# Opening a block of the convolution's kernel behind both slots of a step, its matmul tasks due one step apart

## The chip, the cores and the metric

The kernel runs on one core of a Trainium2 chip. Its engines are TensorE (PE, with its weight loads PEld), VectorE (DVE), ScalarE (ACT), GpSimd (POOL) and SyncE (SP), which here only issues transfers. The metric is the device time of one execution in microseconds (us). Three runs of the kernel before gave 1361.73, 1362.64 and 1366.7 us; their median is 1362.64.

## The reference

Two heads work on separate inputs, and their outputs are set side by side. Head A is a convolution over 2048 positions and 448 channels by a state-space kernel K, made from 256 complex terms for each channel and applied by Fourier transforms. Head B is full softmax attention with 16 heads of 28.

```python
def A(u, log_A_real, A_imag, C_real, C_imag, log_dt, D_skip):      # u: 1 x 2048 x 448
    dt = exp(log_dt)
    A = -exp(log_A_real) + 1j * A_imag                              # 448 x 256
    C = (C_real + 1j * C_imag) * dt[:, None]
    P = exp((A * dt[:, None])[:, :, None] * pos[None, None, :])
    K = 2.0 * einsum("dn,dnl->dl", C, P).real                       # 448 x 2048
    y = irfft(rfft(u_t, 2 * L) * rfft(K, 2 * L), 2 * L)[:, :, :L]
    return y.transpose(0, 2, 1) + u * D_skip

def B(x, wqkv, wo):
    q, k, v = split(x @ wqkv)                                       # 16 heads of 28
    p = softmax(q @ k.T * 28 ** -0.5)
    return (p @ v) @ wo

return concatenate([A(...), B(...)], axis=-1)
```

## The kernel before

The kernel has a prelude and one long loop. The prelude (to about 258 us) projects q, k and v, and makes the first powers ("seeds") for K; both go through DRAM. The loop then runs over 256 steps (`NS`); each step is one tile of 128 keys (`kt`) for a group of four heads and 512 queries (`u`, of which there are 16). Instructions stand on every engine in the order in which the loop writes them.

What a step does is listed in `ORDER`, item by item:

- `m0` to `m3` (`max_mm`) are the four matmuls by which the maximum of later scores is found, 19 steps ahead. Each takes a PSUM tile from a ring of three buffers, called pm in the profile. m0 (weights times `kdif`) is read by a Relu on ACT into `rl`; m1 is joined with that by a custom operation on DVE (`rl<-pm,rl`); m2 and m3 are reduced on DVE (`mx<-pm`).
- `s0` to `s3` (`s_mm`) are the score matmuls into a ring of three other tiles, pss, each followed by the exp on ACT (`p<-pss`).
- `pv` (`pv_step`) multiplies the exps of the step before with v, into po.
- `f` is a slot: one narrow task is run there, if one is due. There are two slots in a step, one ahead of `pv` and one behind it; in the last steps there is a third. A task takes its PSUM tile from the ring pm as well.
- `v` runs the next of a block's nine g operations on DVE (`vec`).
- `k` first has the next block's factors loaded if the current block's powers are all issued (`k_next`), then opens a block if one is due (`k_begin`), and runs up to three of its nine e operations on POOL.

K is made in 56 blocks. A block is opened by `k_start`: three copies on ACT set the first elements of its tables g, e and of the factors zg (zg is one PSUM tile, in which the g operations also keep their scratch). Nine g operations on DVE (the first of them, `lowest`, is three instructions) and nine e operations on POOL then double the tables. After that come three matmul tasks: p0 and m1 (the code's name for p1 and a note that the block is done) multiply g by e, with one copy to `ko` each, and p2 transforms `ko`, with a copy to `yk` on ACT and a store. A block may be opened when its due step (3.5 steps for each block, `KP`) has come, the block two before it is done, and no powers are waiting. The three tasks are put into `m_due` at the opening, and come due `KD` = 5 steps later.

A slot takes the first of these that is due: an urgent task (the end of a maximum, `max_end`; the row sums and the scaling of a finished unit, `sums` and `scale`), an output projection, a task of `m_due`, a u task (a part of the forward transform of u: eight matmuls and one or two evictions on ACT, called ub; these last until step 102), or a task of the spectrum and of the inverse transform (from step 192 on). When all blocks are done, the PSUM pool of pm and zg is replaced by one with four buffers.

Of the kernel before, what the change touches and what calls it, by code (L numbers as in the profile page):

```python
# [30 lines left out]
NU = G * NQ  # L31
NS = NU * NK
LEAD = 3
ORDER = ('m0', 's0', 'm1', 's1', 'v', 'f', 'pv', 'k', 'f', 'v', 'm2', 's2', 'm3', 's3', 'v')
PB = 8
F1 = 2
FX, PD, GAP = 1, 2, 2
# [5 lines left out]
K0, KP, KD, UP = 0, 3.5, 5, 3  # L43
# [47 lines left out]
def body(ctx, tc, a, out):  # L91
# [526 lines left out]
    def k_start(b):  # L618
        sd = sds[b]
        e = g_p.tile([128, 2, 16, N2], F32, name="e", bufs=2)  # L620
        g = g_p.tile([128, 2, 16, N1], F32, name="g", bufs=2)
        zg = ps_g.tile([128, CQ], F32, name="zg")
        egs[b] = e, g
        zgs[b] = zg
        nc.scalar.activation(g[:, :, :, :4], sd[:, F_G:F_Z].rearrange("p (c h e) -> p c h e", c=2, e=4), AF.Copy)
        nc.scalar.activation(zg[:, :Z_G], sd[:, SDF - Z_G:], AF.Copy)
        nc.scalar.activation(e[:, :, :, :8], sd[:, :F_G].rearrange("p (c h e) -> p c h e", c=2, e=8), AF.Copy)

    def e_power(b, i, q):

        t, m = egs[b][0], 8 << i
        zz = sds[b][:, F_Z:].rearrange("p (k f h) -> p k f h", k=6, f=3)
        if q == 0:
            zr = zz[:, i, 0, :][:, None, :, None].to_broadcast([128, 2, 16, m])
            nc.gpsimd.tensor_tensor(t[:, :, :, m:2 * m], t[:, :, :, :m], zr, ALU.mult)
        elif q == 1:
            uts[0] = g_p.tile([128, 2, 16, 32], F32, name="eu")[:, :, :, :m]
            zi = zz[:, i, 1:3, :][:, :, :, None].to_broadcast([128, 2, 16, m])
            nc.gpsimd.tensor_tensor(uts[0], t[:, ::-1, :, :m], zi, ALU.mult)
        else:  # L640
            nc.gpsimd.tensor_tensor(t[:, :, :, m:2 * m], t[:, :, :, m:2 * m], uts[0], ALU.add)

    def g_powers(b):

        t, zg = egs[b][1], zgs[b]
        zz = zg[:, :Z_G].rearrange("p (k f h) -> p k f h", k=3, f=3)
        tt = nc.vector.tensor_tensor

        def first(i, m):
            tt(t[:, :, :, m:2 * m], t[:, :, :, :m], zz[:, i, 0, :][:, None, :, None].to_broadcast([128, 2, 16, m]), ALU.mult)  # L650

        def second(i, m, c):
            n = c.stop - c.start
            u = zg[:, CQ // 2:CQ // 2 + n * 16 * m].rearrange("p (c h m) -> p c h m", c=n, m=m)
            zi = zz[:, i, 1 + c.start:1 + c.stop, :][:, :, :, None].to_broadcast([128, n, 16, m])
            tt(u, t[:, ::-1, :, :m][:, c], zi, ALU.mult)
            return lambda: tt(t[:, c, :, m:2 * m], t[:, c, :, m:2 * m], u, ALU.add)
        both, u = slice(0, 2), {}

        def lowest():  # L660
            first(0, 4)
            second(0, 4, both)()
        ops = [lowest, lambda: first(1, 8), lambda: u.update(a=second(1, 8, both)), lambda: u["a"](), lambda: first(2, 16)]
        for c in (slice(0, 1), slice(1, 2)):
            ops += [lambda c=c: u.update(a=second(2, 16, c)), lambda: u["a"]()]
        return ops
# [3 lines left out]
    def k_mm(b):  # L670
        t_ = {}

        def part0(i):
            pw = w_tile()
            e, g = egs[b] if i == 0 else egs.pop(b)
            for n, (h, c) in enumerate(((0, 0), (0, 1), (1, 0), (1, 1))):
                for j in range(4):
                    x_ = h * 8 + i * 4 + j
                    nc.tensor.matmul(pw[32 * j:32 * j + 32, :N2], g[:, c, x_, :], e[:, c, x_, :],
                                     start=n == 0, stop=n == 3, tile_position=(0, 32 * j))  # L680
            if i == 0:
                t_["ko"] = g_p.tile([128, 2, N2], F32, name="ko", bufs=2)
            nc.scalar.activation(t_["ko"][:, i], pw[:, :N2], AF.Copy)

        def part1():
            ko = t_["ko"]
            pw = w_tile()
            for i in range(2):
                for c in range(2):
                    mm32(pw[64 * c:64 * c + 64, i * 128:(i + 1) * 128], ko[:, i, :], w1[:, c, :], True, True, 64 * c)  # L690
            yk = g_p.tile([128, N1, 4, 2], F32, name="yk", bufs=2)
            nc.scalar.activation(yk.rearrange("p k j i -> p i j k"),
                                 pw[:, :256].rearrange("p (i j k) -> p i j k", i=2, j=4), AF.Copy)
            nc.sync.dma_start(yk_d[b // NBF][:, :, b % NBF], yk.rearrange("p (m k) j i -> p m (k j i)", k=4))
        return [lambda: part0(0), lambda: part0(1), part1]
# [191 lines left out]
    m_due = collections.deque()  # L887
# [71 lines left out]
    def k_begin(s_):  # L959
        if not (k_due and K0 + k_due[0] * KP <= s_ and done["mm"] >= k_due[0] - 2 and not powers["e"] and not powers["g"]):  # L960
            return
        b = k_due.popleft()
        k_start(b)
        powers["g"] += g_powers(b)
        powers["e"] += [lambda i=i, q=q: e_power(b, i, q) for i in range(3) for q in range(3)]
        p0, p1, p2 = k_mm(b)

        def m1():
            p1()
            done["mm"] = b  # L970
        m_due.extend((s_ + KD, t_) for t_ in (p0, m1, p2))
        last[0] = b

    last = [None]
# [13 lines left out]
    for s in range(NS):  # L988
# [25 lines left out]
        ps = []  # L1014
        for op in ORDER:
            if op[0] == "s":
                ps.append(s_mm(u, kt, int(op[1])))
            elif op[0] == "f":
                slot(s)
            elif op[0] == "v":  # L1020
                vec()
            elif op == "k":
                k_next()
                k_begin(s)
                for _ in range(3):
                    if powers["e"]:
                        powers["e"].popleft()()
            elif op == "pv":
                if prev:
                    pv_step(*prev)  # L1030
                    if prev[1] == NK - 1:
                        fin(prev[0], s)
            elif sm < NS:
                max_mm(sm // NK, sm % NK, int(op[1]))
# [76 lines left out]
```

## Time and profile before

| what | before |
|---|---|
| median of three runs | 1362.64 us |
| the profiled execution, device time | 1363.72 us |
| its span in the profile | 1361.9 us |
| mean granted clock of TensorE | 0.976 |
| busy: PE / DVE / ACT / POOL | 1243.9 / 991.3 / 966.1 / 839.5 us |

The span is the time from the first to the last instruction of the program in the profile; the device time contains it and what lies around it. A line of grouped instructions gives the source line (here always L75, a helper that records every operation), the engine, the operation, the tiles that it writes and reads, the shape, the count, then busy time in us and the mean of one in ns, and last the idle time of that engine ahead of them with what ended it. A line of waits gives who waited for whom, the total in us, the number of times and the longest. A line of the chain of waits gives start, length and instruction; a line of the timeline gives start, length, engine and instruction, all in us.

### The profile page before, as it was taken

To read this page: it belongs to the slowest core of one execution; us is meant where nothing else is said; L and a number is where in the kernel's file an instruction comes from. 1 tells how busy PE (TensorE), PEld (TensorE's weight loads), DVE (VectorE), ACT (ScalarE), POOL (GpSimd) and SP (SyncE) were. 2 spreads that over 40 slices of the span, in tenths; PEclk is the share of its full clock that TensorE was granted. 3 is DMA by queue.
4 is the path that set the end of the run, shared out by engine and by line. 5 is a ranking of instruction groups with operands and counts; after the bars stand their busy time and mean duration, and the time that the engine had idled before them with its cause. 6 is when DMAs were issued, how large, how long until landed. Compare 5 with 4: busy or idle time off the path is not lost.

```text
span 1361.9 us, 33142 instructions
## 1 busy us (share of the span) xinstructions
PE 1243.9 (91%) x12625; PEld 709.8 (52%) x12625; DVE 991.3 (73%) x2138; ACT 966.1 (71%) x2067; POOL 839.5 (62%) x705
## 2 busy tenths in 40 slices
PE   6878885799999999999999999999998999998997
PEld 5657762455555555555555555555555545544433
DVE  5897886877777777777788888888887766857311
ACT  4876752488888888888888887878786655655553
POOL 3685681278877878878888988888895111202221
PEclk9988987899999999999999999999999999999999
DMA  6677669636675545378534233632325534636476
GB/s 197 199 261 266 225 212 271 179 74 150 147 164 118 128 135 159 111 202 198 162 94 97 56 73 86 146 79 67 79 65 140 189 116 161 206 111 203 138 192 176
DMA packets 200089, 205.36 MB, mean 151 GB/s; under 512 B 95993, under 2 KB 158521, under 8 KB 197881
## 3 DMA queue, kind: packets, MB, share of 16 engines
q1 hardware_dynamic: 199544, 201.13, 53.2%
q10 hardware_dynamic: 384, 2.10, 0.6%
q8 instruction: 100, 1.64, 0.5%
q14 instruction: 61, 0.49, 0.1%
HBM read 120.73 MB, written 82.18 MB: 149 GB/s over the span
## 4 chain that ended last, share of the span: by engine, by line
PE 61%; DVE 17%; ACT 12%; issue 3%; DMA 3%; POOL 3%; SPq 0%; ACTq 0%; DVEq 0%; POOLq 0%
PE pm L75 35%; PE po L75 13%; PE pss L75 12%; ACT p L75 6%; DVE mx L75 4%; DVE g L75 2%; DVE tri L75 2%; ACT rl L75 2%; DVE p L75 2%; POOL qhat L75 1%; DVE pr L75 1%; DVE zg L75 1%; DVE rl L75 1%; DVE sg L75 1%; ACT tri L75 1%
## 5 line engine op out<-in xcount | busy, mean ns | idle before, releaser
L75 ACT ACTIVATE p<-pss 128x512 f32<-128x512 f32 x1024 | 565.4, 609 | 138.5 <-PE pss L75 127.5
L75 PE MATMUL pss<-qhat,khat 128*128 128x512 f32 x1024 | 403.1, 400 | 3.3 <-ACT p L75 3.3
L75 DVE TENSOR_REDUCE mx<-pm 128x1 f32<-128x512 f32 x500 | 321.4, 683 | 116.3 <-PE pm L75 115.1
L75 PE MATMUL pm<-khat,qhat 128*128 128x512 f32 x749 | 330.1, 444 | 41.4 <-DVE mx L75 36.5
L75 POOL TENSOR_TENSOR e<-e,sdb 128x256 f32<-128x256 f32 x168 | 201.8, 1201 | 171.9 <-ACT e L75 162.9
L75 PE MATMUL po<-p,v 128*32 128x512 f32 x2048 | 271.9, 599 | 0.0
L75 POOL TENSOR_TENSOR e<-e,eu 128x256 f32<-128x256 f32 x168 | 248.1, 1477 | 13.2
L75 PEld LDWEIGHTS pm<-khat,qhat 128*128 128x128 f32 x749 | 142.0, 190 | 216.0 <-DVE mx L75 79.8
L75 PEld LDWEIGHTS pss<-qhat,khat 128*128 128x128 f32 x1024 | 191.1, 189 | 46.7 <-ACT p L75 11.2
L75 DVE CUSTOM_DVE_ANT_0 rl<-pm,rl 128x512 f32<-128x512 f32 x249 | 171.4, 688 | 48.3 <-ACT rl L75 43.8
L75 POOL TENSOR_TENSOR eu<-e,sdb 128x256 f32<-128x256 f32 x168 | 201.7, 1201 | 0.0
L75 DVE TENSOR_TENSOR g<-g,zg 128x128 f32<-128x128 f32 x392 | 162.9, 416 | 46.3 <-ACT zg L75 41.3
L75 ACT ACTIVATE rl<-pm 128x512 f32<-128x512 f32 x249 | 151.2, 607 | 20.7 <-PE pm L75 18.8
L75 POOL TENSOR_TENSOR p<-pr,pr 64x448 f32<-64x448 f32 x32 | 40.9, 1277 | 191.6 <-DVE pr L75 180.5
L75 PE MATMUL pm<-kdif,qhat 128*128 128x512 f32 x249 | 101.6, 408 | 2.2 <-DVE mx L75 1.5
L75 PEld LDWEIGHTS pm<-e,g 128*32 128x32 f32 x3584 | 63.0, 110 | 52.8 <-issue 30.8
L75 DVE TENSOR_TENSOR zg<-g,zg 128x128 f32<-128x128 f32 x224 | 87.5, 391 | 1.9
L75 PEld LDWEIGHTS po<-p,v 128*32 128x32 f32 x2048 | 56.6, 110 | 42.7 <-issue 38.0
L75 PE MATMUL pm<-xh,wh 112*128 112x512 f32 x128 | 56.8, 448 | 22.3 <-DVE hl L75 10.8
L75 PE MATMUL pm<-e,g 128*32 128x64 f32 x3584 | 72.5, 220 | 0.0
L75 ACT ACTIVATE y<-pm 128x448 f32<-128x448 f32 x48 | 26.3, 548 | 63.0 <-PE pm L75 30.7
L75 DVE TENSOR_TENSOR pr<-pm,ub 128x448 f32<-128x448 f32 x64 | 37.0, 619 | 32.7 <-PE pm L75 32.7
(137 smaller groups left out, 1571.8 us busy)
## 6 DMA issues: line engine op xcount, KB each, us to landing
sdb<-sd SPq DMA_DIRECT2D x56, 336.0 KB
qhat<-q SPq DMA_DIRECT2D x64, 256.0 KB
khat<-k SPq DMA_DIRECT2D x56, 256.0 KB
sd<-sg SPq DMA_DIRECT2D x8, 1456.0 KB
k<-hl SPq DMA_DIRECT2D x16, 512.0 KB
q<-hl SPq DMA_DIRECT2D x16, 512.0 KB
mw<-in_mw SPq DMA_DIRECT2D x16, 512.0 KB
sd<-qhat SPq DMA_DIRECT2D x8, 896.0 KB
```

The costliest lines, as they stand in the source:

```text
L75: i = f(*args, **kw)
```

## The change

`ORDER` has `k` behind the second `f` and its `v` instead of between the two slots. And the three tasks of a block come due at 5, 6 and 7 steps after its opening instead of all at 5.

```diff
-ORDER = ('m0', 's0', 'm1', 's1', 'v', 'f', 'pv', 'k', 'f', 'v', 'm2', 's2', 'm3', 's3', 'v')
+ORDER = ('m0', 's0', 'm1', 's1', 'v', 'f', 'pv', 'f', 'v', 'k', 'm2', 's2', 'm3', 's3', 'v')
...
-        m_due.extend((s_ + KD, t_) for t_ in (p0, m1, p2))
+        m_due.extend((s_ + KD + i, t_) for i, t_ in enumerate((p0, m1, p2)))
```

## The prediction

> **What bounds the kernel now.** I read the busy shares first, then the stretches, the waits of TensorE (PE) by stretch, the chain in one step, and the timelines of that step's engines. The page, with the group of ACT's exps:
>
> ```profile
> span 1361.9 us, 33142 instructions
> PE 1243.9 (91%) x12625; PEld 709.8 (52%) x12625; DVE 991.3 (73%) x2138; ACT 966.1 (71%) x2067; POOL 839.5 (62%) x705
> ...
> L75 ACT ACTIVATE p<-pss 128x512 f32<-128x512 f32 x1024 | 565.4, 609 | 138.5 <-PE pss L75 127.5
> ```
>
> PE leads, but its busy time is modelled, so I go by starts of matmuls. The blocks run in two stretches: while the u tasks last (steps 0 to 102), and after them to step 191. The stretches, with the columns PE, PEld, DVE, ACT, POOL, clock, DMA:
>
> ```profile
> 258.00:681.00 423.00, 411.41 (x4760) 224.62 (x4761) 320.76 (x759) 348.99 (x788) 334.45 (x262) 1.00 0.58 144
> 681.00:1020.00 339.00, 319.91 (x3761) 182.24 (x3759) 279.53 (x667) 276.07 (x612) 292.40 (x232) 1.00 0.36 85
> ```
>
> No other engine is full (82% DVE, 81% ACT, 86% POOL in the second) and the granted clock is 1.00, so time lost on PE between matmuls is what can be won. What PE waits for, first in the first stretch, then in the second:
>
> ```profile
> PE pm L75 <- DVE mx L75: 10.1, 20, 1.5
> ```
>
> ```profile
> PE pm L75 <- DVE mx L75: 19.1, 28, 1.3
> ```
>
> One wait carries it all: a max_mm matmul waits for a reduction that frees a buffer of the ring pm, 48 times. Where that happens, the chain in the step that opens block 42 shows (start, us, what):
>
> ```profile
> 855.46 0.19 ACT zg L75
> ...
> 855.68 0.30 DVE g L75
> ...
> 856.62 0.61 DVE mx L75
> ...
> 857.27 0.50 PE pm L75
> ```
>
> The opening's copies on ACT (k_start) release three small DVE operations (`lowest`), and the reduction of m2 stands behind these in DVE's order. m1 of the next step takes the buffer of m2 (ring of three: m2, m3, m0, m1), so PE stands. PE in the same two steps:
>
> ```profile
> 852.46 0.39 PE L75 MATMUL pm<-kdif,qhat 128*128 128x512 f32 x1
> ...
> 852.92 0.39 PE L75 MATMUL pm<-khat,qhat 128*128 128x512 f32 x1
> 853.15 0.40 PE L75 MATMUL pss<-qhat,khat 128*128 128x512 f32 x1
> ...
> 854.91 0.50 PE L75 MATMUL pm<-khat,qhat 128*128 128x512 f32 x1
> ...
> 855.94 0.39 PE L75 MATMUL pm<-kdif,qhat 128*128 128x512 f32 x1
> ...
> 857.27 0.50 PE L75 MATMUL pm<-khat,qhat 128*128 128x512 f32 x1 [0.71 <-DVE mx L75]
> 857.61 0.40 PE L75 MATMUL pss<-qhat,khat 128*128 128x512 f32 x1
> ```
>
> m0 to m1 takes 852.92 - 852.46 = 0.46 us; here 1.33, so 0.87 lost, and the matmul after it starts 0.34 later instead of 0.23: 0.98 in all for 0.71 recorded, 0.27 more than the record. A step with one task p2, and one with empty slots:
>
> ```profile
> 943.55 0.39 PE L75 MATMUL pm<-kdif,qhat 128*128 128x512 f32 x1
> ...
> 945.99 0.50 PE L75 MATMUL pm<-khat,qhat 128*128 128x512 f32 x1
> ...
> 947.03 0.39 PE L75 MATMUL pm<-kdif,qhat 128*128 128x512 f32 x1
> ...
> 950.06 0.39 PE L75 MATMUL pm<-kdif,qhat 128*128 128x512 f32 x1
> ```
>
> 3.48 and 3.03 us: PE back to back, the task costing 0.45. The stall of about 1 us behind an opening is thus all that lies above PE's own work.
>
> **Part 1: the opening behind both slots.** It moves k_start, `lowest` and the first three e operations behind the second slot's task and its `v`; `lowest` now falls to the `v` behind m3. The sum that goes: 10.1 + 19.1 recorded in 48 waits, plus 48 x 0.27, is 42.2 us, 0.88 each. Followed step by step, I put 41 of the 48 behind openings; 7 follow a max_end or a sums task and stay. **Removed: 41 x 0.88 = 36 us.**
>
> Does a new wait take its place? DVE first. In the ordinary step, m2's reduction starts 946.53 - 945.99 = 0.54 after its matmul:
>
> ```profile
> 946.53 1.29 DVE L75 TENSOR_REDUCE mx<-pm 128x1 f32<-128x512 f32 x2 [0.55 <-PE pm L75]
> ```
>
> And DVE and ACT around opening 42, whose order on ACT (yk of a p2, the copies, the exps) is the one that nearly every opening gets after the change:
>
> ```profile
> 853.70 1.11 ACT L75 ACTIVATE p<-pss 128x512 f32<-128x512 f32 x2
> 854.65 0.71 ACT L75 ACTIVATE yk<-pm 128x256 f32<-128x256 f32 x1
> 855.06 0.40 ACT L75 ACTIVATE g<-sdb 128x128 f32<-128x128 f32 x1
> 855.29 0.35 ACT L75 ACTIVATE zg<-sdb 128x144 f32<-128x144 f32 x1
> 855.50 0.46 ACT L75 ACTIVATE e<-sdb 128x256 f32<-128x256 f32 x1
> 855.80 1.13 ACT L75 ACTIVATE p<-pss 128x512 f32<-128x512 f32 x2
> 856.76 0.67 ACT L75 ACTIVATE rl<-pm 128x512 f32<-128x512 f32 x1
> ```
>
> ```profile
> 854.48 0.42 DVE L75 TENSOR_TENSOR g<-g,zg 128x256 f32<-128x256 f32 x1
> ...
> 856.54 1.28 DVE L75 TENSOR_REDUCE mx<-pm 128x1 f32<-128x512 f32 x2
> 857.74 0.41 DVE L75 TENSOR_TENSOR g<-g,zg 128x256 f32<-128x256 f32 x1
> 858.06 0.68 DVE L75 CUSTOM_DVE_ANT_0 rl<-pm,rl 128x512 f32<-128x512 f32 x1
> ...
> 858.67 0.42 DVE L75 TENSOR_TENSOR zg<-g,zg 128x256 f32<-128x256 f32 x1
> 859.13 0.42 DVE L75 TENSOR_TENSOR g<-g,zg 128x256 f32<-128x256 f32 x1
> ```
>
> With the new order m2's reduction starts at 854.91 + 0.54 = 855.45; the two take 857.74 - 856.54 = 1.20, to 856.65. m1's matmul wants its buffer at 855.94 + 0.46 = 856.40; m2 is done at about 856.05: no stall. `lowest` (856.54 - 855.68 = 0.86) runs from 856.65 to 857.51; its zg has been there since 855.64. m1's reduction (`rl`) needs the relu, done at 856.76 + 0.67 = 857.43, so it is 0.1 late. That hides where the next step holds a task. Where its slots are empty (by the planner's rules behind 14 openings), two g operations stand ahead of m2: 857.51 + 0.61 + 0.32 + 0.46 = 858.90, against 855.94 + 2.00 + 0.54 = 858.48 in an unhindered empty step (m2 comes 854.91 - 852.46 = 2.45 into a step with a p2, so 2.00 into an empty one); m2 ends at 859.50, and m1 wanted it at 855.94 + 3.03 + 0.46 = 859.43. With the slow restart 0.25 each: **given back 14 x 0.25 = 3.5 us** (bounds 0 and 0.86 each: none or all of `lowest`; a gain isn't in it, as an empty step has no other loss).
>
> The scratch zg has one buffer: where the block before was opened three steps earlier (half the cases), its last two g operations now end right ahead of the copy of zg: from 854.48 on, 0.46 and 0.42 (the spacing of the rows of 858.67 and 859.13, and the length of the last), to 855.36 against 855.29, 0.1 late; behind it on ACT wait e and the second pair of exps, with 0.17 to spare (end at 856.45; s1 of the next step at 855.94 + 0.69 = 856.63 takes that buffer of pss). The POOL chain starts later by what ACT now does first, at most yk and ub, 1.3 us, and costs 292.40 us for the 26 blocks of the second stretch, 11.2 us each; its p0 comes five steps on, over 15 us. The next block's load on SP (issued in `k`, now behind the second slot's DMAs) has four steps; nothing there comes due.
>
> **Part 2: tasks one step apart.** The same matmuls in other slots: PE work 0 (by 0.45 a task between -2 and +3 us in all). Counted through the planner, openings stay at the same steps, p0, p1 and p2 take mostly the first slot, and a p2 shares the step with 53 openings. The pool of PSUM buffers is changed at step 201 instead of 200, from where the order is as before (2 us either way). The u tasks move into second slots, 17 of them in an opening step, ahead of the copies on ACT, which used to run while PE made the u task:
>
> ```profile
> 405.35 0.94 PE L75 MATMUL pm<-ua,w 128*32 128x448 f32 x8
> ...
> 407.50 0.39 PE L75 MATMUL pss<-qhat,khat 128*128 128x512 f32 x1
> ```
>
> ```profile
> 406.36 0.58 ACT L75 ACTIVATE ub<-pm 128x448 f32<-128x448 f32 x1
> ```
>
> ub can't start before 405.35 + 0.94 = 406.29. Behind it come now 0.74 of copies (855.80 - 855.06): with ub's 0.58 less the overlap of 0.11 shown below, the next exp starts at 406.36 + 0.47 + 0.74 = 407.57 and ends at 408.17, while s1 wanted its buffer at 407.50 + 0.46 = 407.96. With the slow restart 0.32; I take a little more for the u tasks with two evictions: **17 x 0.4 = 6.8 us given back** (bounds 0 and 0.74 + 0.11 each: none or all of the copies).
>
> **Sum.** 36 - 3.5 - 6.8 = 25.7 us. The profiled execution took 1363.72 us (1361.9 span, 1.8 around it), 1.1 over the median of the runs, 1362.64: 1338.0 there, 1337 on the median, where all times below stand.
>
> **The rivals.** *ACT late at openings* (0.15): yk and the copies in one step push the exps back by 0.5 us in the 36 other openings with a p2: 0.5 - 0.17 + 0.11 = 0.44 each, 15.8 us, 1353. For it: ACT waits 127.5 us for pss in the page's row, which are pauses that it may need. Against: in the step of 943.55, with a p2 and no opening, the exps start 946.82 - 943.55 = 3.27 into the step, in the step of opening 42 at 855.80 - 852.46 = 3.34:
>
> ```profile
> 946.82 1.09 ACT L75 ACTIVATE p<-pss 128x512 f32<-128x512 f32 x2 [0.38 <-PE pss L75]
> ```
>
> [...] The trace disagrees: two exps of 0.609 end within 1.11, an overlap of 0.11, and yk starts 0.16 before the second has ended.
>
> *DVE fills up, or the stall has another cause* (0.09): `lowest` only shifts its 0.86 to m1's reduction and the ring stands one tile later; with it the case that the change doesn't do what it says. 1363. Against: DVE busy 279.53 of 339, and the chain above, which runs through `lowest`.
>
> *Slower* (0.08): ACT takes its operations one after the other once it gets no pauses. Relu and four exps of 0.61, yk 0.71 and copies of 1.21 make 4.97 in an opening step against 3.48: 1.49 late, less 0.17, 1.3 in 53 openings, 69 us, for 36 removed and 3.5 given back: 1399. It decides from 0.85 us late (36 / 53 + 0.17). Against: in opening 42, from 853.70 to 855.80, six operations of 3.1 us fit into 2.1.
>
> **How the numbers follow.** The forecast has 0.68. Its own range is 1321 (all 48 waits gone, nothing given back) to 1347 (both give-backs doubled); 1321 to 1356 takes in the ACT rival and leaves out the last two, 0.17, and a little below. Faster by over 0.5% (about what a measurement of this kernel can tell from no change): 0.68 + 0.15 = 0.83; same 0.09; slower 0.08.
>
> **What would show it.** Right: PE's waits for mx in the two stretches fall from 29 to under 8 us; DVE's idle before g for zg is near nothing; the step behind an opening takes 3.5 us, not 4.5; the second stretch gets about 18 us shorter, the first 7. Wrong: pss waiting for p at openings (ACT), rl waiting for the relu by 1 us, or p0 waiting for e of POOL; a gain in the stretch behind step 201 would come from something that I have not seen.

## The result, and the profile after

The changed kernel takes 1342.79 us (median of six, 1340.52 to 1344.13) against 1362.18 for the kernel before in the same comparison (1357.91 to 1366.7): a ratio of 0.9853 [0.9831, 0.9876]. The forecast was 1337.0, the range 1321 to 1356. The profiled execution took 1344.13 us, 19.6 less than the profiled execution before.

The page of the changed kernel, with busy times, the shares of the chain by engine and the group of the maximum's matmuls:

```profile
span 1342.4 us, 33143 instructions
PE 1247.8 (93%) x12625; PEld 706.7 (53%) x12625; DVE 994.4 (74%) x2138; ACT 953.5 (71%) x2067; POOL 838.6 (62%) x705
...
PE 70%; DVE 13%; ACT 6%; DMA 4%; POOL 3%; issue 2%; SPq 1%; ACTq 0%; DVEq 0%; POOLq 0%
...
L75 PE MATMUL pm<-khat,qhat 128*128 128x512 f32 x749 | 328.5, 442 | 15.7 <-DVE mx L75 10.9
```

The same two lines of the kernel before:

```profile
PE 61%; DVE 17%; ACT 12%; issue 3%; DMA 3%; POOL 3%; SPq 0%; ACTq 0%; DVEq 0%; POOLq 0%
...
L75 PE MATMUL pm<-khat,qhat 128*128 128x512 f32 x749 | 330.1, 444 | 41.4 <-DVE mx L75 36.5
```

PE's work is what it was, and the chain runs through PE for 70% of the span, where it had 61%. PE's idle time ahead of these matmuls fell from 41.4 to 15.7 us, 10.9 of it for a reduction. To see where the 19.6 us came from, I cut both profiles where the same steps begin: 0, 102, 191, 201, 224 (and, for the changed kernel, on to the end). Columns as before: length, PE, PEld, DVE, ACT, POOL, clock, DMA share, GB/s. The kernel before:

```profile
258.35:680.79 422.44, 410.85 (x4760) 224.18 (x4758) 320.20 (x758) 348.78 (x787) 334.45 (x262) 1.00 0.58 144
680.79:1019.45 338.66, 319.57 (x3760) 182.06 (x3758) 279.19 (x666) 275.73 (x611) 291.93 (x231) 1.00 0.36 85
1019.45:1065.91 46.46, 42.60 (x562) 24.65 (x560) 32.78 (x67) 31.31 (x67) 22.29 (x17) 0.96 0.48 135
1065.91:1181.80 115.89, 109.36 (x1075) 58.48 (x1074) 85.42 (x149) 70.56 (x138) 20.45 (x17) 1.00 0.52 171
```

The changed kernel:

```profile
257.87:673.63 415.76, 411.01 (x4743) 220.98 (x4742) 322.78 (x759) 343.06 (x786) 334.28 (x262) 1.00 0.60 147
673.63:993.94 320.31, 318.49 (x3775) 180.11 (x3774) 278.36 (x664) 268.25 (x612) 291.13 (x231) 1.00 0.37 88
993.94:1042.61 48.67, 44.80 (x561) 24.82 (x560) 33.43 (x69) 31.55 (x67) 23.48 (x18) 0.93 0.46 138
1042.61:1162.30 119.69, 110.90 (x1075) 58.95 (x1074) 85.51 (x149) 70.64 (x138) 20.45 (x17) 0.99 0.50 163
```

The first stretch is 6.7 us shorter and the second 18.35; the forecast had 7 and 18. The two rows behind them are 2.2 and 3.8 us longer, where the forecast had 2 either way for the pool's change, and the clock there is lower. The prelude is 0.5 shorter, and behind step 224 nothing changed. So the two stretches came out within half a microsecond of it, and nearly all of the miss lies in steps 191 to 224.

What PE waited for, in the first stretch and then in the second:

```profile
PE pss L75 <- ACT p L75: 1.4, 2, 0.9
PE pm L75 <- DVE mx L75: 1.2, 6, 0.2
```

```profile
PE pm L75 <- DVE mx L75: 1.0, 5, 0.2
PE pss L75 <- ACT p L75: 0.5, 2, 0.2
```

The wait that had 29.2 us in 48 places has 2.2 in 11. DVE's waits in the first stretch, of the kernel before and of the changed one:

```profile
DVE g L75 <- ACT zg L75: 25.6, 26, 1.8
DVE rl L75 <- ACT rl L75: 18.1, 48, 0.6
```

```profile
DVE rl L75 <- ACT rl L75: 26.8, 82, 0.9
```

DVE no longer stands before `lowest` for the copy of zg (one wait of 0.8 us is left of 26). It stands a little longer for the relu, spread over 82 places; of that little can reach PE, whose own waits for reductions are the 2.2 us above. The opening of block 42 in the changed kernel, PE first and then DVE:

```profile
836.69 0.39 PE L75 MATMUL pm<-kdif,qhat 128*128 128x512 f32 x1
...
839.14 0.50 PE L75 MATMUL pm<-khat,qhat 128*128 128x512 f32 x1
...
840.17 0.39 PE L75 MATMUL pm<-kdif,qhat 128*128 128x512 f32 x1
840.63 0.39 PE L75 MATMUL pm<-khat,qhat 128*128 128x512 f32 x1
...
843.28 0.39 PE L75 MATMUL pm<-kdif,qhat 128*128 128x512 f32 x1
843.88 0.50 PE L75 MATMUL pm<-khat,qhat 128*128 128x512 f32 x1
844.22 0.40 PE L75 MATMUL pss<-qhat,khat 128*128 128x512 f32 x1
```

```profile
839.67 1.29 DVE L75 TENSOR_REDUCE mx<-pm 128x1 f32<-128x512 f32 x2
840.88 0.28 DVE L75 TENSOR_TENSOR g<-g,zg 128x128 f32<-128x128 f32 x1
...
843.15 1.28 DVE L75 TENSOR_REDUCE mx<-pm 128x1 f32<-128x512 f32 x2
```

m2's reduction starts 0.53 behind its matmul (839.14) and `lowest` comes after it, so m1 of the next step follows m0 by 0.46: no stall. This next step has empty slots, and its two g operations let the next reduction start only at 843.15. It takes 843.28 - 840.17 = 3.11 instead of 3.03, m1 behind it comes 0.60 after m0 instead of 0.46, and s1 0.34 after m1 instead of 0.23: 0.08 + 0.14 + 0.11 = 0.33 is lost, 0.25 of it at m1 and s1. The forecast had 0.25.

### The profile page after: what moved, and what is told of

Its sections match the earlier page's. It is cut to its first block, busy times and chain, and to the rows that moved or that the text cites. A ratio compares the mean times of both kernels' runs of the same rounds, so it can differ in the third digit from the quotient of the medians.

```text
span 1342.4 us, 33143 instructions
## 1 busy us (share of the span) xinstructions
PE 1247.8 (93%) x12625; PEld 706.7 (53%) x12625; DVE 994.4 (74%) x2138; ACT 953.5 (71%) x2067; POOL 838.6 (62%) x705
## 4 chain that ended last, share of the span: by engine, by line
PE 70%; DVE 13%; ACT 6%; DMA 4%; POOL 3%; issue 2%; SPq 1%; ACTq 0%; DVEq 0%; POOLq 0%
PE pm L75 39%; PE po L75 16%; PE pss L75 15%; DVE mx L75 2%; DVE tri L75 2%; ACT p L75 2%; DVE p L75 2%; DVE pr L75 1%; POOL qhat L75 1%; DMA khat<-k 1%; DVE sg L75 1%; DVE px L75 1%; DVE qhat L75 1%; ACT tri L75 1%; DMA q<-hl 1%
## 5 line engine op out<-in xcount | busy, mean ns | idle before, releaser
L75 PE MATMUL pm<-khat,qhat 128*128 128x512 f32 x749 | 328.5, 442 | 15.7 <-DVE mx L75 10.9
L75 PEld LDWEIGHTS pm<-e,g 128*32 128x32 f32 x3584 | 57.4, 110 | 41.5 <-DVE mx L75 18.2
L75 ACT ACTIVATE ub<-pm 128x224 f32<-128x224 f32 (+1 forms) x96 | 38.7, 448 | 39.4 <-PE pm L75 38.3
```

The source lines that it names most:

```text
L75: i = f(*args, **kw)
```

## The experiments

Each was timed beside the kernel before. Two sets shared their runs of it, at 1363.2 us (the first four) and 1363.98 (the last four).

**Half of the change: the order alone**

```diff
-ORDER = ('m0', 's0', 'm1', 's1', 'v', 'f', 'pv', 'k', 'f', 'v', 'm2', 's2', 'm3', 's3', 'v')
+ORDER = ('m0', 's0', 'm1', 's1', 'v', 'f', 'pv', 'f', 'v', 'k', 'm2', 's2', 'm3', 's3', 'v')
```

> The opening behind both slots, the three tasks still due together. Theory (the gain is `lowest` leaving the place ahead of m2's reduction; the 6 us lost behind step 191 come from the pool change one step later, which the spread tasks cause): 36 us removed, 14 empty steps behind an opening give back 0.28 each, 13 openings with a u task in the second slot 0.35 each, nothing lost behind step 191, since the pool is changed at step 200 again: 1336, between 1331 and 1341, faster than the changed kernel. Rival (the spread tasks bring the gain or a good part of it): 1350 or more.

Measured: 1339.52 us (1336.76 to 1345.22), ratio 0.9826 [0.9801, 0.985]. The stages against the kernel before: -6.8, -15.9, +0.4, 0.0 us. The order alone makes the whole gain. The second stretch gains 2.4 less than with the tasks spread. What is slower there is a step with empty slots behind an opening step whose slots are empty too: in seven places it takes 3.52 to 3.55 us from m0 to m0, where the changed kernel takes 3.09 to 3.12. Of the two stages behind it the first loses 0.4, the second nothing.

**The other half: the tasks one step apart, the order as before**

```diff
-        m_due.extend((s_ + KD, t_) for t_ in (p0, m1, p2))
+        m_due.extend((s_ + KD + i, t_) for i, t_ in enumerate((p0, m1, p2)))
```

> The three tasks one step apart, the opening where it was. Theory: the stall of about 1 us stays behind every opening whose second slot holds no u task, so PE's wait for mx in the second stretch stays near 19 us; the pool is changed at step 201, which costs 4 to 6 us: 1362 to 1369. Rival (the spread tasks bring the gain): 1352 or less.

Measured: 1364.59 us (1360.65 to 1366.4), ratio 1.001 [0.9994, 1.0027]: no change. The waits of PE in its second stretch (from 680.5 to 1018.2 us) show the stall still there:

```profile
PE pm L75 <- DVE mx L75: 17.2, 26, 1.2
```

And its step 201 took 7.07 us, where the kernel before took 4.81: here too the pool is changed at 201.

**The changed kernel, with the last block's tasks due together**

```diff
-        m_due.extend((s_ + KD + i, t_) for i, t_ in enumerate((p0, m1, p2)))
+        m_due.extend((s_ + KD + (i if b + 1 < NB else 0), t_) for i, t_ in enumerate((p0, m1, p2)))
```

> The changed kernel, but the last block's three tasks due together, so that the PSUM pool is changed at step 200 again; all else as changed. Theory: the steps 191 to 224 take as long as before the change, 4 to 6 us less than in the changed kernel: 1337 to 1339. Rival (the loss there is the clock, or POOL coming late for the spectrum's join): 1342 to 1344.

Measured: 1335.75 us (1333.27 to 1337.41), ratio 0.9791 [0.9774, 0.9809], 1.3 us below the expected 1337 to 1339. The stages: -6.9, -18.35, +0.5, 0.0. One block of 56 is put back, and the losses in steps 191 to 224 are gone but for 0.5 (step 201 takes 4.82). Not all of that is the block's doing: step 197 comes ahead of the moved tasks, with the same matmuls, and took 8.65 us here and 9.78 in the changed kernel. Its profile also has a prelude 5 us shorter than that of the kernel before, with the same instructions in it.

**The kernel before, with `lowest` alone moved behind m3**

```diff
-ORDER = ('m0', 's0', 'm1', 's1', 'v', 'f', 'pv', 'k', 'f', 'v', 'm2', 's2', 'm3', 's3', 'v')
+ORDER = ('m0', 's0', 'm1', 's1', 'v', 'f', 'pv', 'k', 'f', 'w', 'm2', 's2', 'm3', 's3', 'x')
...
-            elif op[0] == "v":
+            elif op == "v":
+                vec()
+                if len(powers["g"]) == 1:
+                    vec()
+            elif op == "w":
+                if len(powers["g"]) < 9:
+                    vec()
+            elif op == "x":
                 vec()
```

The copies on ACT, the e operations and the tasks stay where they were; only DVE's order at an opening differs.

> The kernel before with `lowest` alone moved: k_start, the e operations and the tasks stay where they were, no g operation runs between the opening and m3, the first runs behind m3, and the last two of a block together in the first `v`. Openings come at the same steps. Theory: the stall goes as in the change, and the copies on ACT run beside the u task again, so nothing is given back for u tasks: 36 less 4 for empty steps, 1330, between 1326 and 1336, the fastest of these. Rival (the copies' place behind the slots or the spread tasks matter): 1345 or more.

Measured: 1336.22 us (1333.98 to 1337.88), ratio 0.9801 [0.9787, 0.9815], 0.2 us outside the expected range of 1326 to 1336. PE's waits for reductions in its first stretch (from 253.1 to 664.8 us), then in its second (to 987.8):

```profile
PE pm L75 <- DVE mx L75: 0.8, 4, 0.2
```

```profile
PE pm L75 <- DVE mx L75: 0.6, 3, 0.2
```

So it was the place of `lowest` ahead of m2's reduction that made the stall; where the copies and the tasks stand needn't change. The first stretch is 10.8 us shorter, 4 more than with the change: the copies stay between the slots, and no exp waits behind both a ub and the copies. The second is 15.6 shorter, with the same slower steps behind empty opening steps that the order alone has (3.53 to 3.55 us in the same seven places).

**The kernel before, its pool of PSUM buffers changed at step 201 instead of 200**

```diff
-        if s >= 12 * NK and f_ready["s", 1] == NS and not (k_due or m_due or powers["g"] or powers["e"]):
+        if s >= 201 and f_ready["s", 1] == NS and not (k_due or m_due or powers["g"] or powers["e"]):
```

> The kernel before, the pool of PSUM buffers changed at step 201 instead of 200, no task moved. Theory (the ring of three at the second spectrum job's join makes PE wait in step 201): step 201 takes 7 to 8.7 us instead of 4.8, all other steps as before: 1365 to 1368. Rival (the changed kernel's long step 201 comes from its order of tasks): no change, 1362 to 1363.

Measured: 1367.82 us (1364.13 to 1369.85), ratio 1.0029 [1.0016, 1.0042]. From step 0 to step 201 no stage differs by more than 0.08 us; step 201 takes 9.78 instead of 4.81, more than the expected 7 to 8.7. Its chain there (start, length, what):

```profile
1059.02 1.17 DVE pr L75 x2
1060.21 1.20 DVE p L75
1061.42 1.46 DVE p L75
1062.88 0.61 DVE mx L75
1063.53 0.79 PE pm L75
```

The same chain in the changed kernel, with the two `p` operations left out:

```profile
1041.49 1.17 DVE pr L75 x2
...
1045.35 0.61 DVE mx L75
1046.01 0.80 PE pm L75
```

With three buffers, m1 of step 201 takes the buffer of m2. m2's reduction stands on DVE behind four operations that join the spectrum, and PE stands for 3 us. In the kernel before, the fourth buffer is there one step earlier, and the same m1 follows s0 without a wait:

```profile
1065.91 0.40 PE L75 MATMUL pss<-qhat,khat 128*128 128x512 f32 x1
1066.14 0.41 PE L75 MATMUL pm<-khat,qhat 128*128 128x512 f32 x1
```

In the changed kernel the last block's p2, due two steps later, falls into step 200, so the pool can only be changed at 201.

**`lowest` alone moved, with the tasks one step apart but for the last block's** (the fourth and the third experiment's lines together)

> `lowest` alone moved, as in the second experiment of that kind, and the tasks one step apart except the last block's. Theory: first stretch as with `lowest` alone (11 us gained), second as in the change (18 us), pool change at step 200: 1333, between 1329 and 1336. Rival (the two gains are one and the same): 1336 as with either.

Measured: 1329.14 us (1327.29 to 1332.55), ratio 0.9757 [0.9736, 0.9778]. The stages: -12.0, -18.65, +0.2, 0.0. This is the change without the losses of the u tasks and of the pool. In the first stretch its tasks stand in the same steps as those of the changed kernel, and it gains 5.3 us more: what the u tasks cost the change.

**The same, all tasks one step apart, and blocks due sooner**

```diff
-K0, KP, KD, UP = 0, 3.5, 5, 3
+K0, KP, KD, UP = 0, 3.4, 5, 3
```

> As the kernel with `lowest` alone moved, with all tasks one step apart, and a block due every 3.4 steps instead of 3.5: the last is opened at step 187, the pool is changed at step 195, ahead of the first spectrum join, and by the planner's rules four fewer tasks stand behind step 255. Theory: the waits of steps 197 and 201 go (3 us each, and the clock's half rate behind them), and the end gets 3 to 5 us shorter: 1323, between 1318 and 1328. Rival (POOL, with 11.6 us a block against 3.4 steps of 3.5 us, now holds p0 back): 1332 or more.

Measured: 1323.13 us (1319.93 to 1325.49), ratio 0.971 [0.9689, 0.9732], the fastest version here, 20 us below the changed kernel. The stages of the second stretch, and of steps 191 to 201:

```profile
666.28:991.35 325.07, 319.75 (x3872) 181.79 (x3870) 282.62 (x675) 269.60 (x615) 299.63 (x237) 0.99 0.36 86
991.35:1034.32 42.97, 41.49 (x481) 24.18 (x480) 31.73 (x57) 30.67 (x61) 9.01 (x7) 1.00 0.62 185
```

The last blocks end sooner: POOL works 9.01 us in steps 191 to 201 instead of 23.48 in the changed kernel, the second stretch holds more matmuls (3872 instead of 3775), and neither step 197 (4.55 us) nor step 201 (4.83) has a stall. Behind step 224 it is some 9 us shorter than the kernel before; which of the later tasks gained that, I didn't follow. The second stretch has a loss that no other run but the next has: in the middle of a product of g and e (p0 or p1), PE stands for 2.95 us without a releaser that the profile shows, and then works one window of 3.41 us at half the clock. Its cause is open.

**The changed kernel with the same `KP` of 3.4**

> The changed kernel with 3.4 steps to a block, nothing else. Theory: the 6 us behind step 191 come back, and steps 197 and the end give 5 to 8 more: 1331, between 1327 and 1336. Rival (POOL holds p0 back): 1342 or more.

Measured: 1331.03 us (1329.81 to 1331.55), ratio 0.9767 [0.9749, 0.9786], 12 us below the changed kernel. The stages: -6.4, -13.0, -3.65, +0.1, and -9.0 behind step 224, as in the run before. The second stretch gains less than in the changed kernel; it too holds more matmuls (3871), and a stall of 2.9 us that nothing in the profile releases. The u tasks' loss in the first stretch stays: it gains 6.4 us where the run before gains 12.3.

## Why the prediction was right, and what it mis-sized

**The stall and its cause: right, and shown.** Moving `lowest` alone takes the wait away (the fourth experiment), moving the tasks alone leaves it (the second). I had left 7 of the 48 waits standing. 11 stand, of 0.2 us each, and none of them behind an opening. What the 41 stalls cost comes out by difference: with `lowest` alone moved and the tasks spread, the two stretches gain 30.65 us, and 14 empty steps at 0.33 give back 4.6, so about 35 us were removed, 0.86 each for the 0.88 of the sum. The change gains 25.0 us there for a sum of 25.7; the term for the empty steps was too small by 1.1 us and the one for the u tasks too large by 1.5, so part of this agreement is luck. Openings didn't all stay at the same steps: three of the 56 moved by one.

**Empty steps: right in kind, a little too small.** 0.25 us each was worked out; the step behind the opening of block 42 shows 0.25 at m1 and s1 behind the empty step, and 0.33 in all. The nine such steps of the second stretch take 4.01 to 4.06 us from their m0 to the next step's s1, instead of 3.03 + 0.46 + 0.23 = 3.72. Without the tasks spread, seven of them stand behind an empty opening step and lose 0.43 more, 3.0 us, where the second stretch of the order alone is 2.4 longer. Why they do was not tested.

**u tasks in opening steps: right in kind, too large.** An opening at step 35 has one eviction behind its u task. PE and ACT:

```profile
400.39 0.94 PE L75 MATMUL pm<-ua,w 128*32 128x448 f32 x8
...
402.75 0.40 PE L75 MATMUL pm<-khat,qhat 128*128 128x512 f32 x1
403.19 0.49 PE L75 MATMUL pss<-qhat,khat 128*128 128x512 f32 x1
```

```profile
401.39 0.54 ACT L75 ACTIVATE ub<-pm 128x448 f32<-128x448 f32 x1 [0.44 <-PE pm L75]
...
402.55 1.07 ACT L75 ACTIVATE p<-pss 128x512 f32<-128x512 f32 x2
```

s1 comes 0.44 behind m1 instead of 0.23, and the exp 1.16 behind ub's start: the copies are in between, as in the forecast. Such an opening loses some 0.32, one with two evictions 0.34 to 0.41, for the 0.4 that I took. Two of the 17 openings lose nothing, and one 0.16. With `lowest` alone moved, the copies stay ahead of ub, and with the tasks in the same steps the first stretch gains 5.3 us more, for the 6.8 of the sum.

**ACT late, DVE full, slower: none came.** PE waits 1.9 us for the exps in both stretches together. In block 42 the exps start 3.47 us into the step instead of 3.34: 0.13 later, within the 0.17 to spare. No matmul of the two stretches waits for POOL. DVE is busy for 278.36 of the 320.31 us of the second stretch, where it was for 279.19 of 338.66.

**The pool's change: the term that was mis-sized.** "The pool of PSUM buffers is changed at step 201 instead of 200, from where the order is as before (2 us either way)" measured 3.8 in step 201, and steps 191 to 201 lost 2.2 more. I had counted the step right, but hadn't asked who needs the fourth buffer in it. The kernel before holds the answer: DVE's operations of the spectrum stand ahead of m2's reduction just there. With the pool's change alone moved, step 201 lost 4.97 us; with the last block's tasks put back, it lost nothing. The clock is part of it. Where the pool is changed at 201, PE stands there for 3.0 us in all three kernels, and what follows differs. The changed kernel, the kernel before with the pool's change moved, and the tasks alone one step apart, in windows of 3.41 us from the one that holds most of the stall (busy PE is the second number, the clock the third from the end):

```profile
1042.51:1045.93 3.42, 0.49 (x3) 0.06 (x1) 3.37 (x5) 1.73 (x4) 2.28 (x2) 1.00 0.06 9
1045.93:1049.34 3.41, 3.33 (x18) 1.20 (x22) 1.32 (x4) 0.60 (x1) 0.00 (x0) 0.50 0.00 0
```

```profile
1059.16:1062.57 3.41, 1.38 (x6) 0.76 (x5) 3.36 (x4) 2.06 (x4) 2.54 (x2) 1.00 0.57 221
1062.57:1065.98 3.41, 2.45 (x10) 0.90 (x14) 2.21 (x5) 0.60 (x1) 0.00 (x0) 0.50 0.00 0
1065.98:1069.40 3.42, 3.42 (x23) 1.76 (x16) 0.52 (x1) 0.58 (x2) 0.00 (x0) 0.50 0.00 0
```

```profile
1062.67:1066.08 3.41, 1.65 (x10) 1.04 (x6) 3.23 (x4) 2.06 (x4) 2.43 (x2) 1.00 0.25 38
1066.08:1069.50 3.42, 2.18 (x26) 0.97 (x26) 2.48 (x5) 0.60 (x1) 0.10 (x1) 1.00 0.00 0
```

The stall alone costs step 201 7.07 - 4.81 = 2.3 us, with one window at half the clock 3.8, with two 4.97. So "2 us either way" was the size of the stall without the clock, but the prediction had no stall in it. Of the 2.2 us ahead of step 201, 1.7 fall in step 197, which has a stall in both kernels (2.51 us before, 2.94 after) and takes 9.78 us instead of 8.10; there the clock is at half for two windows instead of one. The other 0.5 falls in steps 198 to 200, where the last block's tasks stand. Without what steps 191 to 224 lost, and the 0.5 of the prelude, the profiled execution would have taken 1344.13 - 6.0 + 0.5 = 1338.6 us, for a forecast of 1338.0.

So the change as made isn't shown to be better than its first half. The spreading wins 2.4 us in the second stretch and loses 3.8 at step 201; the medians are 1342.79 and 1339.52, the ratios 0.9853 and 0.9826, and their intervals overlap.

## What to carry to other kernels

Where an engine runs in order and frees a ring of buffers, put small work that waits for a third engine behind the operations that free the ring; here three operations of 0.3 us each held up TensorE for about 0.86 us in 41 places. Look next at the places where a change only moves a boundary (a pool that is changed, a last block that ends a step later): ask which instruction of that step needs what the boundary brings, for one such step gave back 3.8 of the 25 us won. And a wait in an otherwise full TensorE can cost more than its record says: 0.27 us more at the wait of 0.71 that was followed here, and behind one of 2.5 to 3 us none, one or two windows of 3.41 us at half the clock.

## What the runs showed of the hardware

**At a stall of 2.5 to 3.5 us the granted clock was 0.50 for 3.41 us, for 6.83 us, or not at all.** From 259.31 to 1047.79 us of the kernel before, which is all of its two stretches but the first microsecond, with its 41 stalls of 0.9 us, the clock was 1.00. From 260 to 1339 us it left 1.00 five times in the two kernels, each time in a stall of PE or within 1.6 us behind one. Step 197 of the kernel before, with a stall of 2.51 us, and of the changed kernel, with one of 2.94:

```profile
1044.37:1047.79 3.42, 0.81 (x3) 0.30 (x2) 3.37 (x4) 1.91 (x4) 2.36 (x2) 1.00 0.50 198
1047.79:1051.20 3.41, 3.25 (x18) 1.12 (x22) 1.40 (x4) 0.60 (x1) 0.00 (x0) 0.50 0.00 0
```

```profile
1018.62:1022.03 3.41, 1.07 (x4) 0.30 (x2) 3.35 (x4) 2.17 (x4) 2.54 (x2) 1.00 0.14 22
1022.03:1025.45 3.42, 2.57 (x10) 0.90 (x14) 2.09 (x5) 0.60 (x1) 0.00 (x0) 0.50 0.00 0
1025.45:1028.86 3.41, 3.41 (x24) 1.78 (x17) 0.63 (x1) 0.69 (x2) 0.00 (x0) 0.50 0.00 0
```

The other three are step 201 of the changed kernel (a stall of 3.00 us, rows above) and, in each kernel, a wait of 3.51 us for DVE's `ot` (at 0.50 from 1232.11 us before and from 1213.18 after); behind these three it was 0.50 for 3.41 us. In the 3.41 us ahead of the five drops PE was busy for 0.81, 1.07, 0.49, 0.94 and 1.50 us, by the profile's modelled times.

At step 201 the stall of 3.0 us was followed by 3.41 us at 0.50 in one kernel, by 6.83 us in another, and by none in a third (the seven rows of the three kernels above). Step 197 too, with the same matmuls, took 6.61 us with a stall of 2.5 us and no drop (the tasks alone one step apart), 8.10 with 3.41 us at half the clock (the kernel before), and 9.32 with 6.83 us (`lowest` alone moved); with a stall of 2.94 it took 8.65 with 3.41 us (the last block's tasks put back), 9.52 and 9.78 with 6.83 us (the order alone, and the changed kernel). So the length of a stall alone doesn't tell what followed it; what does, no run here was made to test.

**The prelude isn't the same length each time.** It has the same instructions in all of these kernels, and TensorE's clock in it differs. The order alone, and then the tasks alone one step apart:

```profile
0.00:252.40 252.40, 194.55 (x783) 143.74 (x784) 200.57 (x369) 148.72 (x293) 134.58 (x159) 0.91 0.75 238
```

```profile
0.00:258.75 258.75, 202.46 (x783) 151.31 (x784) 200.57 (x369) 148.86 (x293) 134.52 (x159) 0.86 0.74 232
```

6.35 us apart at 0.91 and 0.86, with the same DVE time to 0.01 us. The runs of the kernel before differ by up to 8.8 us (1357.91 to 1366.7), so this may be much of their spread; that the clock is its cause, and not what stands with it, no run here shows.
